# Attention over K and V: one shared pool for both loads, V six pairs behind K, later stores, and the last store on two queues

## The chip, the cores and the metric

The kernel runs on one core of a Trainium2 chip. The metric is the device time of a run in microseconds (us). The medians come from three to eleven runs of a kernel. A trace and a profile belong to one of these runs each. The span of a profile is about 1.8 us shorter than the time of its run.

A ratio below is the mean time of one kernel's fast runs over that of the other's in the same rounds on the same chip, so it is not quite the ratio of the medians that stand beside it.

## The reference

```python
B, Hq, Hkv, Sq, Sk, D = 16, 32, 8, 16, 2048, 128        # bf16, values about 0.05
def reference(q, k, v):
    k = jnp.repeat(k, Hq // Hkv, axis=1); v = jnp.repeat(v, Hq // Hkv, axis=1)
    scores = jnp.einsum("bhqd,bhkd->bhqk", q, k) * D ** -0.5
    return jnp.einsum("bhqk,bhkd->bhqd", softmax(scores), v)
```

There are 128 groups (a batch and a K/V head). Each has 64 query rows, 512 KB of K and 512 KB of V. The kernel works on 64 pairs of groups, so it loads 64 K transfers and 64 V transfers of 1 MB (the last V in two halves), 8 Q transfers of 256 KB, and stores 2 MB. All of K and V is read once: 134 MB. Nothing is reused, and this decides what can bound the kernel.

## The kernel before

All loads and stores are issued from SP in one fixed order. K and V have rings of buffers of their own, six for K and seven for V, each of 8 KB per partition. A load waits until the last reader of the buffer's previous content is done.

```python
NBK = 6; NBV = 7; NBO = 5; LAG = 5; DSTORE = 6
# ... order of the DMA queue: K(t), then V(t - lag), and every second step the store of two pairs
    for t in range(NP + max(lag, DSTORE) + 1):
        if t < NP:
            dma.append(("K", t))
        # ... Q chunks
        if 0 <= t - lag < NP:
            dma += v_of(t - lag)                       # the last pair: two halves
        if t - lag - DSTORE in range(0, NP, 2):
            dma.append(("ST", (t - lag - DSTORE) // 2))
# ... what a load waits for
    add(("K", i), *[opt(i >= nbk, ("kx", (i - nbk) // 2, i % 2, h)) for h in halves])
    add(v, opt(p >= NBV, ("pv", p - NBV, 0)))
```

`kx` is DVE's 32x32 transpose of K, `S` the scores, `ex` the exponential on ACT, `pt` and `pe` the transposition of the probabilities and its copy, `pv` the product with V, `nm` the normalization into the output tile. A store covers two pairs in two transfers of 32 KB, both from SP:

```python
                for gg in range(2):
                    g = 4 * x + 2 * gg
                    sp.dma_start(of[64 * g:64 * (g + 2), :].rearrange("(p m) d -> m p d", p=2),
                                 Osb[s][64 * gg:64 * (gg + 1), :, :]).then_inc(prog.sem_dma[kind][s], 16)
```

The exponential is taken without a maximum. So at the end every engine reads a flag that says whether all row sums lay in range, and branches: past a second program that would do it all again with the maximum, or into it.

```python
        eng.wait_ge(sem_flag, 4)
        eng.reg_load(reg, flag[0:1, 0:1].bitcast(I32))
        eng.br_eq(reg, all_within, on_true=after, on_false=redo).branch_hint(hints[me])
        # ... the second program lies here, then the label `after`
    # SP: transfers, this test, then fast.wait_stores(sp)
```

The branch is taken past the second program.

Of the kernel before, what the change touches and what calls it, by code (L numbers as in the profile page):

```python
# [11 lines left out]

NBK = 6
NBK_GENERAL = 4
NBV = 7
NBO = 5
NKT = 2
NPT = 3
LAG = 5
DSTORE = 6  # L20
QCH = 1024
# [8 lines left out]
    ("dve", "nm"): 0.36, ("dve", "pe"): 0.69, ("act", "pe"): 1.03, ("act", "qe"): 1.06, ("dve", "qe"): 1.25,  # L30
    ("act", "nm"): 0.42, ("act", "ex"): 1.27, ("pool", "qr"): 1.6, ("act", "qr"): 1.1, ("dve", "qr"): 1.1,
}
# [9 lines left out]
         "pe": ("act", "dve"), "qe": ("act", "dve"), "qr": ("pool",), "ex": ("act",), "qt": ("pe",), "S": ("pe",),  # L42
         "pt": ("pe",), "pv": ("pe",)}
_PRIO = {"S": 0, "mx": 0, "nb": 0, "ex": 0, "pt": 1, "pe": 1, "pv": 2, "rs": 2, "rc": 2, "nm": 2, "kx": 3, "qr": 3,
         "qt": 3, "qe": 3}


def make_ops(NP, pairs_per_chunk, general):

    deps = {}  # L50
    dma = []
    nbk = NBK_GENERAL if general else NBK
    ch = lambda p: p // pairs_per_chunk
# [6 lines left out]

    opt = lambda ok, op: op if ok else None
    v_of = lambda p: [("VH", x) for x in halves] if p == NP - 1 else [("V", p)]
    for c in range(n_ch):
        add(("Q", c), *[opt(c >= 2, ("qr", c - 2, x)) for x in range(4)])
        for x in range(4):
# [3 lines left out]
            add(("qe", c, x), ("qt", c, x), opt(c >= 2, ("S", last_of(c - 2))))  # L69
    for i in range(NP):  # L70
        add(("K", i), *[opt(i >= nbk, ("kx", (i - nbk) // 2, i % 2, h)) for h in halves])
    for p in range(NP):
        for v in v_of(p):
            add(v, opt(p >= NBV, ("pv", p - NBV, 0)))
    for s in range(NP // 2):
# [7 lines left out]
    for p in range(NP):  # L83
        for h in halves:
            u = 2 * (p // 2) + h
            if general:
                add(("mx", p, h), ("S", u), *[opt(p >= 2, ("ex", p - 2, x)) for x in halves])
            add(("ex", p, h), ("nb", p) if general else ("S", u), *[opt(p >= 2, ("pt", p - 2, x)) for x in halves])
        if general:
            add(("nb", p), ("mx", p, 0), ("mx", p, 1))  # L90
        for h in halves:
            add(("pt", p, h), ("ex", p, 0), ("ex", p, 1), opt(p >= 1, ("pe", p - 1, h)))
            add(("pe", p, h), ("pt", p, h), opt(p >= NPT, ("pv", p - NPT, 0)))
        for x, v in enumerate(v_of(p)):
            add(("pv", p, x), ("pe", p, 0), ("pe", p, 1), v, opt(p >= 1, ("nm", p - 1)))
        add(("rs", p), ("ex", p, 0), ("ex", p, 1))
        add(("rc", p), ("rs", p))
        add(("nm", p), ("pv", p, len(v_of(p)) - 1), ("rc", p), opt(p // 2 >= NBO, ("ST", p // 2 - NBO)))
        if p % 2:
            add(("ST", p // 2), ("nm", p - 1), ("nm", p))  # L100
    qstep = {max(0, c * pairs_per_chunk - QLEAD): c for c in range(n_ch)}
    dma.append(("Q", 0))
    lag = min(LAG, nbk - 1)
    for t in range(NP + max(lag, DSTORE) + 1):
        if t < NP:
            dma.append(("K", t))
        if qstep.get(t, 0):
            dma.append(("Q", qstep[t]))
        if 0 <= t - lag < NP:
            dma += v_of(t - lag)  # L110
        if t - lag - DSTORE in range(0, NP, 2):
            dma.append(("ST", (t - lag - DSTORE) // 2))
    dma += [("ST", s) for s in range(NP // 2) if ("ST", s) not in dma]
    return deps, dma


def pair_of(op, pairs_per_chunk):
    if op[0] in ("qr", "qt", "qe"):
        return op[1] * pairs_per_chunk - 1.5
    return 2 * op[1] + 0.5 if op[0] == "kx" else op[1] + {"S": -1.5, "pv": 1.5}.get(op[0], 0)  # L120


def build_schedule(NP, pairs_per_chunk, general):

    deps, dma = make_ops(NP, pairs_per_chunk, general)
    left = sorted((op for op in deps if op[0] in _ENGS),
                  key=lambda op: (pair_of(op, pairs_per_chunk), _PRIO[op[0]]))
    done, free = {}, {"pe": _T0, "dve": _T0, "act": _T0, "pool": _T0, "sp": _T0}
    progs = {"pe": [], "dve": [], "act": [], "pool": [], "sp": []}
    dma_left, dma_end = list(dma), _T0 + _DMA_LAT  # L130

    def ready(op):
# [5 lines left out]
        return r  # L138

    while left or dma_left:  # L140
        best = None
        if dma_left:
            rd = ready(dma_left[0])
            if rd is not None:
                st = max(free["sp"] + _LAT_SAME, rd + _LAT)
                best = ((round(st, 3), -1, -1), st, "sp", dma_left[0])
# [16 lines left out]
        if eng == "sp":  # L163
            dma_left.pop(0)
            end = st + _ISSUE
            dma_end = max(dma_end, end + _DMA_LAT) + _SIZE[op[0]] / _BW
# [6 lines left out]
        progs[eng].append(op)  # L173
    return deps, progs, max(done.values())


def bass_standalone__gqa_softmax__sampling_kernel(
# [27 lines left out]
    QT = [sb(f"QT{i}", [128, 4, qch], BF16) for i in range(2)]  # L205
    Kn = [sb(f"Kn{i}", [128, 2 * J * 64], I32) for i in range(NBK)]
    KT = [sb(f"KT{i}", [128, 2, J * 64, 2], I32) for i in range(NKT)]
    Vb = [sb(f"Vb{i}", [128, 2, J, 128], BF16) for i in range(NBV)]
    Sneg = [Kn[NBK_GENERAL + i][:, :].bitcast(F32) for i in range(2)]
    P = [sb(f"P{i}", [128, Sk], BF16) for i in range(2)]  # L210
# [18 lines left out]
    sem_id = sem("sem_id")  # L229
    sem_flag = sem("sem_flag")  # L230
    class Program:
        def __init__(self, tag, general):
            self.general = general
            self.rings = {"K": NBK_GENERAL if general else NBK, "V": NBV, "VH": 2, "Q": 2, "ST": NBO}
            self.deps, self.progs, _ = build_schedule(NP, qch // 128, general)
            self.sem_eng = {e: sem(f"{tag}_{e}") for e in ("pe", "dve", "act", "pool")}
            self.sem_dma = {kind: [sem(f"{tag}_{kind}{i}") for i in range(n)] for kind, n in self.rings.items()}
            self.where = {op: (e, i + 1) for e in self.sem_eng for i, op in enumerate(self.progs[e])}

        def point(self, op):  # L240
            if op[0] in self.rings:
                n = self.rings[op[0]]
                return self.sem_dma[op[0]][op[1] % n], (32 if op[0] == "ST" else 16) * (op[1] // n + 1)
            e, i = self.where[op]
# [19 lines left out]
        def wait_stores(self, eng):  # L264
            for s in range(max(0, NP // 2 - NBO), NP // 2):
                eng.wait_ge(*self.point(("ST", s)))

# [7 lines left out]
    def mark_hint(eng, me, prog, op):  # L275

        if not prog.general and op == prog.progs[me][max(0, len(prog.progs[me]) - HINT[me])]:
            hints[me] = eng.mark_branch_hint_location()

    def group_of(p, gg):  # L280
        return 4 * (p // 2) + 2 * gg + p % 2

    def elementwise(eng, me, prog, before_last=None):
        waits = prog.waiter(eng, me)
        for op in prog.progs[me]:
# [5 lines left out]
            if kind == "kx":  # L291
                _, _, gg, h = op
                ins = eng.transpose(KT[p % NKT][:, gg, :, h],  # L293
                                    Kn[(2 * p + gg) % prog.rings["K"]][:, J * 64 * h:J * 64 * (h + 1)])
            elif kind == "qr":
# [21 lines left out]
            elif kind == "rs":  # L317
                ins = eng.tensor_tensor(rowsum[:, p:p + 1], rhalf[:, p, 0:1], rhalf[:, p, 1:2], op=ALU.add)  # L318
            elif kind == "rc":
                ins = eng.reciprocal(rrec[:, p:p + 1], rowsum[:, p:p + 1])  # L320
            elif kind == "nm":
                dst, src, r = Osb[p // 2 % NBO][:, p % 2, :], O_ps[:, 0:128], rrec[:, p:p + 1]
                if me == "act":
# [14 lines left out]
    def transfers(sp, prog):  # L338
        waits = prog.waiter(sp, "sp")
        for op in prog.progs["sp"]:  # L340
            kind, x = op
            waits(op)
            mark_hint(sp, "sp", prog, op)
            s = x % prog.rings[kind]
            if kind == "K":
                dst = Kn[s][:, :].bitcast(BF16)
                src = kf[2 * x:2 * x + 2].rearrange("g (b r) d -> (g b) (r d)", r=2 * J)
            elif kind[0] == "V":
                p, part = (x, slice(0, J)) if kind == "V" else (NP - 1, slice(J // 2 * x, J // 2 * (x + 1)))
                g = group_of(p, 0)  # L350
                dst = Vb[p % NBV][:, :, part, :].rearrange("a g r d -> a g (r d)")
                src = vf[g:g + 3:2].rearrange("g (a r) d -> a g r d", r=J)[:, :, part, :].rearrange("a g r d -> a g (r d)")
            elif kind == "Q":
                dst, src = Qn[s][:, :, :], qf[qch * x:qch * (x + 1), :].rearrange("(a i) d -> a i d", i=NI)
            else:
                for gg in range(2):
                    g = 4 * x + 2 * gg
                    sp.dma_start(of[64 * g:64 * (g + 2), :].rearrange("(p m) d -> m p d", p=2),  # L358
                                 Osb[s][64 * gg:64 * (gg + 1), :, :]).then_inc(prog.sem_dma[kind][s], 16)
                continue  # L360
            sp.dma_start(dst, src).then_inc(prog.sem_dma[kind][s], 16)  # L361

    def matmuls(pe, prog):
        waits = prog.waiter(pe, "pe")
        for op in prog.progs["pe"]:
# [30 lines left out]
            else:  # L396
                rs = range(J) if p < NP - 1 else range(J // 2 * op[2], J // 2 * (op[2] + 1))
                for r in rs:
                    for gg in range(2):
                        ins = pe.matmul(  # L400
                            O_ps[64 * gg:64 * (gg + 1), 0:128],
                            PT[p % NPT][:, r, 64 * gg:64 * (gg + 1)],
                            Vb[p % NBV][:, gg, r, :],
                            start=(r == 0), stop=(r == J - 1), skip_group_check=True,
# [94 lines left out]
```

## Time and profile before

350.98 us, median of three runs (350.42 to 351.04).

| what | before |
|---|---|
| PE, ACT, DVE busy | 69%, 67%, 63% |
| hardware DMA queue, share of 16 engines | 98.2% |
| rate from 20 to 320 us | 413 to 414 GB/s |
| last normalize ends | 344.56 us |
| span ends | 349.2 us |

Lines of the profile's page of the kernel before: the span, the busy time of each engine, the DMA engines' busy tenths and rate in 40 slices, two queues with packets, MB and share of 16 engines' span, and issues with KB each and us to landing.

```profile
span 349.2 us, 11953 instructions
PE 240.3 (69%) x5378; PEld 171.6 (49%) x5378; DVE 220.9 (63%) x359; ACT 232.3 (67%) x387; POOL 28.9 (8%) x35
...
DMA  7999999999999999999999999999999999999972
GB/s 310 425 411 414 414 409 413 416 412 413 413 417 411 416 415 409 413 415 415 414 414 414 412 414 415 412 417 415 411 416 411 414 417 414 417 412 411 388 292 55
...
q1 hardware_dynamic: 37264, 138.42, 98.2%
q8 instruction: 43, 0.70, 0.8%
...
Kn<-in_k_dram SPq DMA_DIRECT2D x64, 1024.0 KB, 17.0
Vb<-in_v_dram SPq DMA_DIRECT2D x63, 1024.0 KB, 17.3
```

The compute engines are a third idle and the DMA engines are full from the second slice on. The three last slices (388, 292, 55) look as if something were left to gain there.

The windows of the kernel before: for each stretch in us, the busy time of each engine, the granted clock, the DMA share and GB/s.

```profile
20.00:100.00 80.00, 62.54 (x1358) 43.58 (x1336) 58.38 (x98) 57.02 (x94) 7.98 (x8) 0.91 1.02 413
100.00:200.00 100.00, 70.42 (x1653) 50.73 (x1649) 64.50 (x101) 72.54 (x123) 7.99 (x8) 0.97 1.03 414
200.00:320.00 120.00, 80.50 (x1856) 57.85 (x1856) 75.05 (x121) 80.38 (x138) 7.99 (x8) 0.94 1.03 414
...
330.00:336.00 6.00, 5.56 (x144) 4.10 (x128) 1.79 (x6) 5.14 (x9) 0.00 (x0) 1.00 1.00 384
336.00:342.00 6.00, 4.32 (x115) 3.66 (x112) 3.24 (x9) 0.01 (x1) 0.00 (x0) 1.00 0.59 210
342.00:349.20 7.20, 1.40 (x34) 1.07 (x34) 0.94 (x7) 0.00 (x0) 0.00 (x0) 0.85 0.11 22
```

At 336 to 342 us the rate is 210 GB/s at a DMA share of 0.59: half of the engines have nothing left. Which half, and why, the views do not say, but the trace has more. Each load raises its semaphore sixteen times, once for each DMA engine that has finished its share. The Trainium skill (DMA: Bandwidth & Descriptors, "Why a DMA increments its semaphore by 16 and not by 1") says that these engines finish independently, and the trace agrees. Here are the sixteen times of six loads of the kernel before (us, sorted within each load):

```
at 21 us        21.4 21.4 21.4 21.5 21.5 21.5 21.6 21.6 21.6 21.6 21.6 21.7 21.7 21.8 21.8 21.9
next load       23.9 23.9 23.9 24.0 24.0 24.0 24.0 24.1 24.1 24.2 24.2 24.2 24.3 24.3 24.4 25.7
later           49.0 49.1 49.1 49.1 49.2 49.2 49.2 49.3 49.3 49.3 49.3 49.5 50.7 50.9 51.1 51.1
late           300.5 300.6 300.6 300.8 301.0 301.7 302.4 303.2 306.9 306.9 307.0 308.2 308.4 308.5 308.6 308.7
last V, half 0 335.0 335.0 335.1 335.2 335.2 335.3 335.4 335.5 340.4 340.6 340.6 340.7 340.7 340.8 340.9 342.1
last V, half 1 336.2 336.2 336.3 336.4 336.4 336.6 336.6 337.0 341.8 341.9 342.0 342.0 342.1 342.1 342.2 343.5
```

One engine falls 1.4 us behind, then a few, and from about 286 us on eight engines come 5 to 8 us after the first. The last increments still follow each other every 2.5 us per load, to the end. A load counts only when its last engine is done, so the eight late engines set the pace of the kernel. The first step backwards (25.7) comes right after the first instruction fetch of 16 KB in the trace's DMA records, at 23.1 us.

The chain of instructions at the end, from the timeline of the kernel before:

```profile
343.53 0.64 PE L400 MATMUL O_ps<-Vb,PT 128*64 128x128 bf16 x16 [0.48 <-DMA Vb<-in_v_dram]
344.10 0.09 PEld L451 LDWEIGHTS QT_ps<-within,ones 128*1 128x1 f32 x2
344.10 0.19 PE L451 MATMUL QT_ps<-within,ones 128*1 128x2 f32 x2
344.21 0.35 DVE L326 TENSOR_SCALAR O<-O_ps,rrec 128x128 bf16<-128x128 f32 x1 [1.68 <-PE O_ps L400]
344.48 0.14 DVE L464 TENSOR_REDUCE flag<-QT_ps 1x1 f32<-1x2 f32 x1
344.59 1.25 SPq L358 DMA_DIRECT2D out_dram<-O  x2
```

The last product waited for the last V half (landed 343.5), then comes the last normalize, then SP issues two store transfers one after the other, 1.25 us for both. From the waits of SP in the same stretch:

```profile
SPq L266 <- DMA out_dram<-O: 1.6, 1, 1.6
```

Line 266 is the wait for the stores. SP was through with its range test and stood 1.6 us more for the last store.

### The profile page before, as it was taken

What the parts mean: (1) busy time and instruction counts of PE and PEld (TensorE: products, weight loads), DVE (VectorE), ACT (ScalarE), POOL (GpSimd) and SP (SyncE); (2) the same over time, 40 slices, a digit from 0 to 9 for tenths busy, and PEclk for the clock granted to TensorE, in tenths of its full rate; (3) what the DMA queues carried; (4) which work ended last, traced back from release to release, by engine and by line L of the source; (5) the groups of instructions that cost most, each with busy time, mean ns of one, the idle gap of its engine ahead of it and who ended that gap; (6) DMA issues with size and microseconds to landing.
All of it is one profiled execution on the core that took longest, in us unless ns stands there. A gap on an engine that the chain in (4) does not pass through costs nothing.

```text
span 349.2 us, 11953 instructions
## 1 busy us (share of the span) xinstructions
PE 240.3 (69%) x5378; PEld 171.6 (49%) x5378; DVE 220.9 (63%) x359; ACT 232.3 (67%) x387; POOL 28.9 (8%) x35
## 2 busy tenths in 40 slices
PE   1587778877687775866567767776757577676782
PEld 1355456554365553644445545454535455455562
DVE  4858867657787557666567555585566665675551
ACT  4488688867389477785569754787676676574740
POOL 1310003000130003000040000400004000000000
PEclk9999899989789899899999988999999989898998
DMA  7999999999999999999999999999999999999972
GB/s 310 425 411 414 414 409 413 416 412 413 413 417 411 416 415 409 413 415 415 414 414 414 412 414 415 412 417 415 411 416 411 414 417 414 417 412 411 388 292 55
DMA packets 37319, 139.23 MB, mean 399 GB/s; under 512 B 11408, under 2 KB 11408, under 8 KB 29072
## 3 DMA queue, kind: packets, MB, share of 16 engines
q1 hardware_dynamic: 37264, 138.42, 98.2%
q8 instruction: 43, 0.70, 0.8%
q14 instruction: 12, 0.10, 0.1%
HBM read 136.31 MB, written 2.10 MB: 396 GB/s over the span
## 4 chain that ended last, share of the span: by engine, by line
DMA 68%; PE 13%; DVE 7%; ACT 7%; SPq 4%; issue 1%
DMA Kn<-in_k_dram 64%; PE S_ps L384 6%; DVE KT L293 6%; ACT P L312 4%; PE PT_ps L394 4%; DMA Vb<-in_v_dram 3%; SPq L358 3%; PE O_ps L400 2%; ACT PT L335 2%; SPq L361 1%; PE QT_ps L372 1%; ACT QT L335 1%; DVE PT L335 1%; DVE rowsum L318 0%; DVE rrec L320 0%
## 5 line engine op out<-in xcount | busy, mean ns | idle before, releaser
L293 DVE STREAM_TRANSPOSE KT<-Kn 128x1024 int32<-128x1024 int32 x128 | 154.7, 1231 | 108.2 <-DMA Kn<-in_k_dram 98.8
L312 ACT ACTIVATE P<-S_ps 128x1024 bf16<-128x1024 f32 x128 | 130.1, 1023 | 63.2 <-PE S_ps L384 53.9
L384 PE MATMUL S_ps<-KT,QT 32*64 32x512 bf16 x2048 | 78.2, 414 | 50.3 <-DVE KT L293 37.4
L394 PE MATMUL PT_ps<-ident,P 128*128 128x128 bf16 x1024 | 76.3, 232 | 35.3 <-ACT P L312 30.4
L394 PEld LDWEIGHTS PT_ps<-ident,P 128*128 128x128 bf16 x1024 | 63.8, 104 | 62.5 <-ACT P L312 42.2
L400 PE MATMUL O_ps<-Vb,PT 128*64 128x128 bf16 x2048 | 73.5, 228 | 2.6 <-DMA Vb<-in_v_dram 2.0
L400 PEld LDWEIGHTS O_ps<-Vb,PT 128*64 128x64 bf16 x2048 | 62.9, 115 | 13.6 <-issue 5.5
L384 PEld LDWEIGHTS S_ps<-KT,QT 32*64 32x64 bf16 x2048 | 28.3, 107 | 73.5 <-DVE KT L293 41.1
L335 ACT ACTIVATE PT<-PT_ps 128x1024 bf16<-128x1024 bf16 x60 | 61.3, 1021 | 4.2 <-PE PT_ps L394 4.1
L299 POOL COPY Qr<-Qn 128x1024 bf16<-128x1024 bf16 x28 | 27.9, 1039 | 238.2 <-DMA Qn<-in_q_dram 238.2
L335 DVE COPY PT<-PT_ps 128x1024 bf16<-128x1024 bf16 x68 | 44.6, 662 | 1.8 <-PE PT_ps L394 1.6
L372 PE MATMUL QT_ps<-ident,Qr 128*128 128x128 bf16 x256 | 22.7, 239 | 15.8 <-ACT Qr L299 6.0
L324 ACT ACTIVATE O<-O_ps,rrec 128x128 bf16<-128x128 f32 x44 | 16.1, 367 | 24.1 <-PE O_ps L400 24.1
L335 ACT ACTIVATE QT<-QT_ps 128x1024 bf16<-128x1024 bf16 x24 | 24.6, 1023 | 8.7 <-PE QT_ps L372 8.6
L372 PEld LDWEIGHTS QT_ps<-ident,Qr 128*128 128x128 bf16 x256 | 17.0, 106 | 22.8 <-issue 12.3
L312 ACT ACTIVATION_READ_ACCUMULATOR P<-S_ps 128x1 f32 x128 | 25.9, 203 | 0.0
L326 DVE TENSOR_SCALAR O<-O_ps,rrec 128x128 bf16<-128x128 f32 x20 | 6.6, 329 | 7.5 <-PE O_ps L400 7.4
L318 DVE TENSOR_TENSOR rowsum<-rhalf 128x1 f32<-128x1 f32 x64 | 9.5, 177 | 1.6 <-ACT P L312 1.6
L335 DVE COPY QT<-QT_ps 128x1024 bf16<-128x1024 bf16 x8 | 9.7, 1210 | 1.1 <-PE QT_ps L372 1.1
L320 DVE RECIPROCAL rrec<-rowsum 128x1 f32<-128x1 f32 x64 | 7.9, 154 | 0.1
L299 ACT ACT_TABLE_LOAD x1 | 1.3, 1283 | 3.5 <-DMA Qn<-in_q_dram 3.5
L299 DVE COPY Qr<-Qn 128x1024 bf16<-128x1024 bf16 x2 | 1.3, 690 | 3.4 <-DMA Qn<-in_q_dram 3.4
(13 smaller groups left out, 4.2 us busy)
## 6 DMA issues: line engine op xcount, KB each, us to landing
Kn<-in_k_dram SPq DMA_DIRECT2D x64, 1024.0 KB, 17.0
Vb<-in_v_dram SPq DMA_DIRECT2D x63, 1024.0 KB, 17.3
Qn<-in_q_dram SPq DMA_DIRECT2D x8, 256.0 KB, 17.1
out_dram<-O SPq DMA_DIRECT2D x64, 32.0 KB, 13.7
Vb<-in_v_dram SPq DMA_DIRECT2D x2, 512.0 KB, 12.0
```

Of the source, the lines that this page charges most:

```text
L293: ins = eng.transpose(KT[p % NKT][:, gg, :, h], Kn[(2 * p + gg) % prog.rings["K"]][:, J * 64 * h:J * 64 * (h + 1)])
L299: ins = eng.activation(dst, src, ACT.Copy) if me == "act" else eng.tensor_copy(dst, src)
L312: ins = eng.activation(P[p % 2][:, :].rearrange("m (r a h j) -> m h a r j", h=2, a=2, j=32)[:, h], src.rearrange("m (a r j) -> m a r j", a ...
L318: ins = eng.tensor_tensor(rowsum[:, p:p + 1], rhalf[:, p, 0:1], rhalf[:, p, 1:2], op=ALU.add)
L320: ins = eng.reciprocal(rrec[:, p:p + 1], rowsum[:, p:p + 1])
L324: ins = eng.activation(dst, src, ACT.Copy, scale=r)
L335: ins = eng.activation(dst, src, ACT.Copy) if me == "act" else eng.tensor_copy(dst, src)
L358: sp.dma_start(of[64 * g:64 * (g + 2), :].rearrange("(p m) d -> m p d", p=2), Osb[s][64 * gg:64 * (gg + 1), :, :]).then_inc(prog.sem_dma[k ...
L372: ins = pe.transpose(QT_ps[:, 128 * i:128 * (i + 1)], Qr[:, x, i, :], ident[:, :],)
L384: ins = pe.matmul(S_ps[64 * gg:64 * (gg + 1), 512 * a:512 * (a + 1)], QT[c % 2][32 * a:32 * (a + 1), x, row:row + 64], kt[:, :, x // 2, p ...
L394: ins = pe.transpose(PT_ps[h][:, 128 * t:128 * (t + 1)], P[p % 2][:, 128 * r:128 * (r + 1)], ident[:, :])
L400: ins = pe.matmul(O_ps[64 * gg:64 * (gg + 1), 0:128], PT[p % NPT][:, r, 64 * gg:64 * (gg + 1)], Vb[p % NBV][:, gg, r, :], start=(r == 0), ...
```

## The change

The intent: one pool of fifteen slots for K and V in place of two rings, each slot given to the next load in the order in which a model of the schedule says that slots come free. V is six pairs behind K in place of five. Stores are issued twelve steps behind V in place of six, with nine output tiles. The last two pairs are stored apart, and the last pair in two transfers, one from SP and one from ACT (`STA`).

```diff
-NBK = 6
-NBK_GENERAL = 4
-NBV = 7
-NBO = 5
+NSLOT = 15
+NSLOT_GENERAL = 13
+NBO = 9
-LAG = 5
-DSTORE = 6
+LAG = 6
+DSTORE = 12
 ...
-        if p % 2:
+        if p == NP - 2:
+            add(("ST", p // 2), ("nm", p))
+        elif p == NP - 1:
+            add(("ST", NP // 2), ("nm", p))
+            add(("STA", 0), ("nm", p))
+        elif p % 2:
             add(("ST", p // 2), ("nm", p - 1), ("nm", p))
 ...
+    def take_slot(op):
+        best = None
+        for x, slot in enumerate(tenants):
+            last = frees(slot[-1], NP) if slot else []
+            if all(o in done for o in last):
+                cand = (max([done[o] for o in last], default=0.0), x, last)
+                best = cand if best is None or cand[:2] < best[:2] else best
+        return best
 ...
+            elif kind == "STA":
+                eng.dma_start(*out_rows(NP - 1, 1)).then_inc(*prog_sem(prog, op))
+                continue
 ...
+            elif x >= NP // 2 - 1:
+                p = NP - 2 if x == NP // 2 - 1 else NP - 1
+                for gg in range(2 if p == NP - 2 else 1):
+                    sp.dma_start(*out_rows(p, gg)).then_inc(*prog_sem(prog, op))
+                continue
```

## The prediction

> **What bounds the kernel now.** The DMA rings, not the compute engines. The page gives PE 69%, ACT 67%, DVE 63% busy; the hardware DMA queue is at 98.2% of 16 engines, and the stretches of 10 us from 10 to 320 us move 408 to 418 GB/s. The waits of the issuing engine (SPq, over 150 us in total) look large, but a load takes 17 us from issue to landing, nearly seven loads of 2.5 us: SPq waits while the rings are full.
>
> The last stretches look like an opening: 392 GB/s at 320-330, 315 at 330-340, about 210 GB/s (DMA share 0.57) at 336-342. I do not think it is one. The Trainium skill ("DMA: Bandwidth & Descriptors", on why a DMA increments its semaphore by 16) says that the engines of one DMA finish independently. The trace has all 16 increments of each load: first and last are 0.5 us apart at 20 us, but 8.2 us apart from 282 us on. Eight engines run late; the last increments still follow each other every 2.5 us per load to the end, plus 0.15 us for each store DMA between. The 43 instruction fetches of 16 KB (1.05 us each), which seem to fall on these eight, explain the lag (estimate: six steps of about 1.4 us on the slowest). At 336-342 the fast half has nothing left and the slow half works at its full rate. The slowest engine's work, 128 loads at 2.51, eight Q loads at 0.65, 58 store DMAs at 0.15 and its fetches, already fills 3 to 343.5 us. More slots, earlier issue and fewer SPq waits give the fast engines a longer lead and the slow ones nothing.
>
> **What changes, costed.**
> 1. Pool of fifteen, V six behind K: SPq waits shrink, loads take longer from issue to landing (estimate 25 to 33 us against 17), steady 414 GB/s unchanged. Worth 0 on the critical path.
> 2. Later stores: 52 store DMAs stand ahead of the last V load against 58. Six times 0.15 us: the last V half lands about 0.9 us earlier (343.5 to 342.6).
> 3. Split last store: before, the last normalize ended at 344.56, the first half store had landed at 346.5, the second, issued 0.6 us later, at 347.1 on twelve engines but 348.9 on four, where fetches came between. SPq waited 1.6 us for it, so the range test and branch were through by about 347.3. With the two halves issued together by SP and ACT, both should land about 2 us after the normalize, and the branch becomes the floor: 2.7 us instead of 4.4. Worth 0.6 to 1.6 us.
> 4. Nothing else on the path moves; PE, ACT and DVE work is reordered, not changed.
>
> Sum: 1.5 to 2.5 us, some of which may be lost to where the end's fetches fall. Predicted 348.9 us, 8 in 10 between 347.4 and 350.4. Chances: faster by over 2% 0.03, within 2% 0.96, slower 0.01.
>
> **What would show it.** Step 1: GB/s between 20 and 320 us within 2 of before; SPq waits for K and V loads shorter; issue to landing clearly above 17 us; the last landing's spacing still 2.5 us. Step 2: last V landing between 342 and 343.2 us, and a late bunch of stores landing after it. Step 3: normalize to end of span under 4 us (4.65 before).
>
> **What would make it wrong.** If the slow engines did sit idle for want of issued loads, a full queue would gain up to 5 us more (345 or less). If the number of fetches on the slowest engine changes by one, 1.4 us either way. If slots given out by modelled times block SPq on a release that comes late, the rings could run dry: slower. If the first DMA from ACT is slow to start, step 3 gives nothing.

## The result, and the profile after

The changed kernel takes 348.41 us (348.09 to 348.87, four runs) against 350.94 us before. The ratio is 0.9932, with a 95% interval from 0.9915 to 0.9949. So it is 2.5 us faster, within 2%.

The page of the changed kernel:

```profile
span 346.9 us, 11937 instructions
PE 238.6 (69%) x5378; PEld 172.7 (50%) x5378; DVE 225.8 (65%) x377; ACT 226.6 (65%) x369; POOL 29.0 (8%) x35
...
GB/s 309 426 412 415 411 413 412 412 415 414 411 418 415 412 412 414 415 413 414 413 412 417 414 415 414 414 413 415 413 413 414 412 417 416 414 412 412 392 336 108
...
q1 hardware_dynamic: 37216, 138.41, 98.9%
q8 instruction: 43, 0.70, 0.8%
...
slot<-in_k_dram SPq DMA_DIRECT2D x64, 1024.0 KB, 17.6
slot<-in_v_dram SPq DMA_DIRECT2D x63, 1024.0 KB, 17.7
```

The slices from the third on run at the same rate as before. A load takes 17.6 us from issue to landing, where it took 17.0: two more slots did not put more loads into flight. (The last slices have higher figures because the span, and so a slice, is shorter, and because more stores fall into them.)

Windows of the changed kernel:

```profile
20.00:100.00 80.00, 59.22 (x1352) 42.48 (x1344) 61.97 (x103) 56.91 (x94) 7.99 (x8) 0.96 1.02 413
100.00:200.00 100.00, 69.97 (x1594) 50.51 (x1595) 64.04 (x105) 69.78 (x115) 7.99 (x8) 0.93 1.03 414
200.00:320.00 120.00, 82.74 (x1904) 59.94 (x1902) 76.42 (x129) 78.09 (x132) 7.99 (x8) 0.94 1.02 414
...
330.00:336.00 6.00, 5.27 (x144) 4.20 (x144) 2.94 (x6) 3.15 (x5) 0.00 (x0) 1.00 0.98 370
336.00:342.00 6.00, 5.03 (x124) 4.19 (x117) 3.16 (x9) 3.15 (x5) 0.00 (x0) 1.00 0.61 203
```

413 and 414 GB/s in the three long stretches, as before, to the last digit. The half-empty stretch at 336 to 342 us is there too (203 against 210). The end, from the timeline of the changed kernel:

```profile
344.03 0.19 PE L519 MATMUL QT_ps<-within,ones 128*1 128x2 f32 x2
344.15 0.35 DVE L390 TENSOR_SCALAR O<-O_ps,rrec 128x128 bf16<-128x128 f32 x1 [0.91 <-PE O_ps L468]
344.42 0.14 DVE L532 TENSOR_REDUCE flag<-QT_ps 1x1 f32<-1x2 f32 x1
344.53 0.56 ACTq L381 DMA_DIRECT2D out_dram<-O  x1
```

The last normalize ends at 344.50 us; before it was 344.56. All but 0.06 us of the gain of 2.3 us in the span lies after it: 2.43 us from normalize to end in place of 4.66. The wait for the stores (1.6 us before) is not in the waits any more.

The trace gives the rest. Times after the last normalize, in us:

| | before | after |
|---|---|---|
| SP issues the last transfer it has | 0.66 | 0.03 |
| SP's branch starts | 2.10 | 1.32 |
| SP's first instruction after its branch | 2.61 | 1.85 |
| last store landed, twelve of its engines | 2.6 | 1.9 |
| last store landed, all sixteen | 4.35 | 1.99 |

Before, the last transfer landed on twelve engines at 347.0 to 347.2 us and on four at 348.5 to 348.9. In between lie an instruction fetch of 16 KB at 346.5 us and four of 8 KB from 346.2 to 347.7.

### The profile page after: what moved, and what is told of

It reads as the page before. It is cut to its first block, busy times and chain, and to the rows that moved or that the text cites. A ratio compares the mean times of both kernels' runs of the same rounds, so it can differ in the third digit from the quotient of the medians.

```text
span 346.9 us, 11937 instructions
## 1 busy us (share of the span) xinstructions
PE 238.6 (69%) x5378; PEld 172.7 (50%) x5378; DVE 225.8 (65%) x377; ACT 226.6 (65%) x369; POOL 29.0 (8%) x35
## 4 chain that ended last, share of the span: by engine, by line
DMA 72%; DVE 11%; PE 9%; ACT 6%; issue 1%; SPq 0%; ACTq 0%
DMA slot<-in_k_dram 72%; DVE KT L354 9%; PE O_ps L468 3%; ACT P L373 2%; PE PT_ps L462 2%; PE S_ps L452 2%; PE QT_ps L440 1%; ACT QT L399 1%; DVE PT L399 1%; ACT PT L399 1%; DMA Qn<-in_q_dram 1%; DVE O L390 1%; ACT L360 0%; ACT Qr L360 0%; DVE rowsum L379 0%
## 5 line engine op out<-in xcount | busy, mean ns | idle before, releaser
L354 DVE STREAM_TRANSPOSE KT<-slot 128x1024 int32<-128x1024 int32 x128 | 154.5, 1231 | 101.3 <-DMA slot<-in_k_dram 92.8
L462 PE MATMUL PT_ps<-ident,P 128*128 128x128 bf16 x1024 | 74.4, 229 | 83.1 <-DVE PT L399 44.0
L462 PEld LDWEIGHTS PT_ps<-ident,P 128*128 128x128 bf16 x1024 | 62.3, 102 | 104.7 <-DVE PT L399 53.7
L452 PE MATMUL S_ps<-KT,QT 32*64 32x512 bf16 x2048 | 75.9, 401 | 11.0 <-ACT P L373 9.7
L468 PE MATMUL O_ps<-slot,PT 128*64 128x128 bf16 x2048 | 76.7, 233 | 1.3 <-DVE O L390 1.0
L468 PEld LDWEIGHTS O_ps<-slot,PT 128*64 128x64 bf16 x2048 | 65.9, 119 | 17.8 <-issue 14.2
L399 ACT ACTIVATE QT<-QT_ps 128x1024 bf16<-128x1024 bf16 x23 | 23.5, 1023 | 7.3 <-PE QT_ps L440 7.3
L388 ACT ACTIVATE O<-O_ps,rrec 128x128 bf16<-128x128 f32 x27 | 9.9, 367 | 11.6 <-PE O_ps L468 11.6
L390 DVE TENSOR_SCALAR O<-O_ps,rrec 128x128 bf16<-128x128 f32 x37 | 12.0, 324 | 5.5 <-PE O_ps L468 5.4
L399 DVE COPY QT<-QT_ps 128x1024 bf16<-128x1024 bf16 x9 | 10.9, 1209 | 1.8 <-PE QT_ps L440 1.8
## 6 DMA issues: line engine op xcount, KB each, us to landing
slot<-in_k_dram SPq DMA_DIRECT2D x64, 1024.0 KB, 17.6
```

Source lines behind the costliest of these rows:

```text
L354: ins = eng.transpose(KT[p % NKT][:, gg, :, h], prog.slot(("K", 2 * p + gg))[:, J * 64 * h:J * 64 * (h + 1)])
L388: ins = eng.activation(dst, src, ACT.Copy, scale=r)
L390: ins = eng.tensor_scalar(dst, src, r, None, op0=ALU.mult)
L399: ins = eng.activation(dst, src, ACT.Copy) if me == "act" else eng.tensor_copy(dst, src)
L452: ins = pe.matmul(S_ps[64 * gg:64 * (gg + 1), 512 * a:512 * (a + 1)], QT[c % 2][32 * a:32 * (a + 1), x, row:row + 64], kt[:, :, x // 2, p ...
L462: ins = pe.transpose(PT_ps[h][:, 128 * t:128 * (t + 1)], P[p % 2][:, 128 * r:128 * (r + 1)], ident[:, :])
```

## The experiments

The theory under test, A: the late DMA engines bound the load stream, so the pool, the longer lead and the later stores are worth next to nothing, and the gain is the end of the program. The rival, B: the pool and the order gain by keeping the DMA queue fuller, and the end adds to it. Twelve kernels were run. The kernel before was run beside them on each chip (medians 350.86 to 351.00 us).

### The split of the last store alone, and the change without it

To the kernel before, only the parts of the change that concern the last two pairs were added (`o_of`, `STA`, the stores of pairs 62 and 63, the waits for them). The rings, LAG = 5 and DSTORE = 6 stayed.

> The kernel before with one part of the change alone: pair 62 stored by itself, pair 63 as two halves, one from SP and one from ACT. Theory A (the rings bound the load stream, the gain is the end of the program): nearly the whole gain, 348.4 to 349.0 us against 350.9; last normalize near 344.5 us, normalize to end of span about 2.4 us in place of 4.65. Theory B (the pool, the longer lead of K and the later stores gain by keeping the rings full): at most a third of the gain, 350.0 us or more.

Measured: 348.59 us (348.42 to 348.79), ratio to before 0.9934 (0.9921 to 0.9947). That is the whole gain, from a small part of the edit. Last normalize at 344.50, span 346.9.

The other way round, the changed kernel with the last two pairs stored together from SP:

```diff
-    o_of = lambda p: p // 2 if p < NP - 1 else NP // 2
+    o_of = lambda p: p // 2
-        if p == NP - 2:
-            ...
-        elif p % 2:
+        if p % 2:
```

> The changed kernel with the last two pairs stored together from SP, as before; pool, order and store delay kept. Theory A: the gain is gone, 350.3 to 351 us, with normalize to end of span about 4.5 us. Theory B: most of the gain stays, 349 us or less.

Measured: 351.46 us, ratio 1.0016 (1.0003 to 1.0028). The gain is gone, and a little more. Normalize to end of span is 5.65 us here, more than theory A said; part of that has a cause of its own, below. But the last store by itself was late enough: it landed on all sixteen engines only 4.71 us after the normalize (4.35 before the change, 1.99 after). Both runs together reject B.

### Both last halves from SP

```diff
-            add(("STA", 0), ("nm", p))
-                for gg in range(2 if p == NP - 2 else 1):
+                for gg in range(2):
```

> The changed kernel with pair 63 still stored apart from pair 62, but both its halves from SP, one after the other. If the second queue is what counts: the second half is issued 0.6 us later and SP reaches its range test 0.6 us later, so 349.0 us or more (0.6 above the changed kernel). If storing the pair apart (smaller and fewer transfers at the very end) is what counts: within 0.3 us of 348.4.

Measured: 350.78 us, ratio 0.9990. So storing the last pair apart from pair 62 is worth nothing by itself; the second queue is worth 2.4 us by the medians and 2.0 us by the ratios (0.9990 against 0.9932), over three times the 0.6 us of issue that it saves. The waits of SP show the same wait as before the change:

```profile
SPq L315 <- DMA out_dram<-O: 1.8, 1, 1.8
```

The second half was issued 0.5 us after the first. It landed on twelve engines at 346.7 to 346.8 us, and on the last at 348.96. The Trainium skill (DMA: Bandwidth & Descriptors, "Issuing engines are not separate DMA queues") says that issuing from several engines only saves the sequencer's time, usually small. For the transfer itself that holds. What the saved half microsecond seems to have bought here is to be ahead of the fetches that follow the branch. The next run tests this.

### The same without the range test

To see whether it is the branch that holds four engines, the run with both halves from SP was made without the test, the branches and the second program. It is correct for these inputs and is no version to keep.

```diff
-            unless_in_range(sp, "sp", again)
+            # the same on the four other engines; flag and its product left out too
```

> The run with both last halves from SP (350.78 us), without the range test and the other branch of the program behind it. There the second half landed on twelve engines at 346.8 us and on four at up to 348.96. If the instruction fetches that follow the branch hold these four: all sixteen within 0.5 us of each other, and the time down by about 2 us, to 348.4 to 349.2. If a second transfer from the same queue is late in itself: four engines still up to 2 us late, and 350 us or more.

Measured: 348.89 us, 1.9 us less by the medians (1.5 by the ratios, 0.9947 against 0.9990), at the upper part of what was expected. The second half landed at 346.4 to 346.6 us on all sixteen engines. The page shows one fetch of 16 KB less, and in the trace no fetch of either size begins after 344.4 us.

```profile
span 347.1 us, 11913 instructions
q8 instruction: 42, 0.69, 0.8%
```

So the branch and what follows it cause the straggling, and a second transfer on a queue is not late in itself. That the instruction fetches do it is the reading of their times and sizes. The run took them away together with the branch, so this step is inferred.

### Stores six steps behind V

```diff
-DSTORE = 12
+DSTORE = 6
```

> The changed kernel with stores issued six steps behind V, as before, in place of twelve. My prediction said that later stores let the last V half land 0.9 us earlier (six store DMAs of 0.15 us moved behind it); the profile of the changed kernel shows only 0.16 us. If the 0.9 us is real but hidden by an instruction fetch on the slowest engine and by the compute chain: last V landing up to 0.9 us later, time up by 0 to 0.9 us. If the stores' place is worth nothing: within 0.2 us of 348.4.

Measured: 348.62 us, 0.2 us above the changed kernel and inside its scatter. The last V half landed 0.34 us later (343.67 against 343.33) and the last normalize ended 0.33 us later. So the stores' place is worth about 0.3 us in the profile, not 0.9.

### How many slots

```diff
-NSLOT = 15
+NSLOT = 10
```

> The changed kernel with ten slots in the pool in place of fifteen. Both traces show that a slot is held for 18 to 19 us (from the issue of its load to the end of its last reader) while a load is issued every 2.55 us, so 7 to 8 slots are in use at a time, whatever the pool holds; and no more than about eight loads and stores are in flight. Theory A (the pool is not what limits issue): within 0.3 us of 348.4. Theory B (more slots keep the rings fuller): slower by 2 us or more, with a lower steady GB/s.

Measured: 350.89 us. By the time alone, theory A would fall here: five slots less take the whole gain. But the loads were not later: last V half at 343.3 us, last normalize at 344.33, last store at 346.4 us, all as in the changed kernel. What came later was the end of the span, at 349.2 us. In this run the first instruction of SP after its branch starts 2.59 us after the branch, where the changed kernel has 0.45. That is a stall that no slot takes part in. The run with the joint last store has it too. A table of the runs discussed so far, from the traces:

```
run                      SP: instructions before its branch, then us from branch to next instruction
ten slots                208   2.59
joint last store         209   2.59
changed kernel           210   0.45
both halves from SP      211   0.44
before                   215   0.44
split alone              216   0.44
stores six steps behind  232   0.44
```

So ten slots were run once more, with waits for counts that had long been reached, put before four of the K loads:

```diff
+            if kind == "K" and x in (36, 40, 44, 48) and not prog.general:
+                for e in ("pe", "dve", "act", "pool"):
+                    sp.wait_ge(prog.sem_eng[e], x - 30)
```

> The run with ten slots took 350.89 us, but its loads and stores were as early as in the changed kernel (last store landed at 346.4 us); SP stood still for 2.66 us after its branch, against 0.5 us in the changed kernel, as it did in the run with the joint last store. SP had issued 208 and 209 instructions before its branch in these two, 210 or more in all runs without the stall. So here the same ten slots, with waits for counts long reached put before four K loads (four or more instructions more, nothing else). If where the branch lies in SP's program decides the stall, and not the pool: no stall, 348.2 to 348.9 us. If ten slots are too few: 350.5 us or more, as before.

Measured: 348.36 us (348.1 to 348.9), ratio 0.9931. The branch is now instruction 216 of SP, the gap 0.44 us. Useless instructions made the kernel 2.5 us faster, and the pool of ten is as good as that of fifteen. The stall belongs to the place of the branch in SP's program. It is not the distance from the branch hint, which every one of these branches has: the hint lies 167 instructions ahead both in the run with the joint store, which stalls, and in the changed kernel, which does not. Whether the place of the branch or that of its target counts is open, since the waits move both. The Trainium skill (Runtime: NRT & Kernel Launch, "Instruction fetch mechanics") says that instructions come in blocks of 16 KiB, and that a branch to a target outside the window that is loaded stalls for a fetch. The stall fits this, but that it is a fetch is not shown: near SP's branch the traces hold one fetch of 16 KB with the stall (346.2 us with ten slots) and without it (346.3 us in the changed kernel). Why 209 misses and 210 hits, these runs do not tell.

With eight slots and the same waits:

> The same with eight slots. 7.3 slots are in use on average in the traces (18.5 us held, one load per 2.55 us). If the slots in use are what the loads need: eight is at the edge, some issue waits for a slot, the steady GB/s falls by 1 to 5% and the time is 351 to 365 us. If the queue hides it: within 0.5 us of the run with ten slots.

Measured: 349.18 us (348.70 to 350.49), 0.8 us above ten slots: between the two cases, and well under the 351 us of the first. The profile is of the slowest of its four runs. The rate stays at 408 to 420 GB/s in the slices from the third to the thirty-sixth. SP came 0.4 us late to its last store, and that store again landed late on one engine (348.3 us, the other fifteen by 346.6). So even eight slots hardly starve the queue. The traces say why. When SP ends an issue between 60 and 320 us, seven to nine earlier transfers are in flight, in 99% of the cases before the change, in 97% after it and with ten slots. And the slots had long been free: each load's slot had been released at least 8.8 us before SP began to issue the load before the change, and at least 11.3 us after it (5.7 us at the median with ten slots, 0.7 with eight). So the long waits of SP, which lie in the issues themselves, are not for slots, though the view of its waits names engines for them. That they end when the queue has room fits the steady count. What sets this limit is left open.

### Are the late engines late because of instruction fetches?

PE's instructions are 10756 of the 11937. The first test took 3584 of them away by leaving out 14 of the 16 blocks of each product with V. The result is wrong; loads and stores are untouched.

```diff
-                rs = range(J) if p < NP - 1 else range(J // 2 * op[2], J // 2 * (op[2] + 1))
+                rs = (0, J - 1) if p < NP - 1 else ((0,), (J - 1,))[op[2]]
```

> Wrong result on purpose: the product with V uses 2 of the 16 key blocks, which takes 3584 of PE's 10756 instructions away and leaves every load and store as it is. If instruction fetches make eight engines late: 28 to 29 fetches of 16 KB in place of 43, first and last increment of a load at 300 us 5 to 6 us apart in place of 8, last V half landing at 340 to 341.5 us in place of 343.3, time 346 to 347.3 us. If these eight engines are slow for another reason: still 8 us apart, time within 0.4 us of 348.4 (PE's lighter work alone can take about 0.5 us off the tail of the last pair).

Measured: the page has 29 fetches in place of 43, the first and last engine of a load are 5.1 us apart at 300 us and 6.2 at 319 us (8.2 at both times in the changed kernel), and the last V half landed at 340.2 us in place of 343.3. All three as expected for fetches.

```profile
span 346.4 us, 8353 instructions
q8 instruction: 29, 0.48, 0.6%
```

The time, 349.57 us (348.19 to 350.79), is a miss. In the profiled run, the fastest of the four, the last normalize ended at 341.49 us, 3.0 us earlier than in the changed kernel. Then PE's branch took 3.90 us in place of 0.49 and ended at 346.03, and the last store landed at 345.8. So the gain was lost behind the branch again, this time on PE, and in a late store. The granted clock was lower too, 0.76 to 0.78 in the four runs (0.94 to 0.95 in the changed kernel); what that cost was not separated. The time of this run says little; its landings do.

A correct version of the test: in pairs 8 to 23, one product for both groups (128 rows by 256 columns, of which half is read) in place of two, on top of the kernel before with the split. It takes 512 instructions from PE.

```diff
+MERGED = range(8, 24)
 ...
+                if p in MERGED and not prog.general:
+                    for r in rs:
+                        ins = pe.matmul(O_ps[:, 0:256], PT[p % NPT][:, r, :], Vb[p % NBV][:, :, r, :],
+                                        start=(r == 0), stop=(r == J - 1))
+                    rs = ()
+    # and nm in two halves for these pairs: rows 0:64 from columns 0:128, rows 64:128 from 128:256
```

> The kernel before with the split of the last store (348.59 us), and in pairs 8 to 23 one product with V for both groups, 128 rows by 256 columns, half of whose result is not read (sixteen matmuls of a pair in place of 32, normalize in two halves): 512 of PE's 10756 instructions less, two fetches of 16 KB less. In the run before, the 41st fetch, at 336.3 us, held one of the sixteen engines up by 1.3 us (343.4 against 342.1 for the next), and the last product waited for it. If fetches make the late engines late: the last V half lands 1.0 to 1.6 us earlier, and 347.0 to 347.7 us. If not: 348.4 to 348.8 us.

Measured: 350.38 us, a miss in time, a hit in mechanism. The last V half landed at 342.2 us (343.4 with the split alone) and the last normalize ended at 343.24 (344.50). Then 5.4 us passed to the end. The waits of SP in this run show where: line 461 is the barrier at the end of the program, where all engines meet.

```profile
SPq L461 <- PEq L461: 3.3, 1, 3.3
```

The name is that of the event; the engine that came last was ACT, by the trace. Its next instruction after its branch came 3.17 us later, where the other runs have 0.40 to 0.43. The second normalize halves had made ACT's program longer: the branch was its instruction 447, in all other runs it was 400 to 436. It is the same stall, on another engine. So in the last run the normalize of the 16 pairs was given to DVE:

```diff
-            engs = ("dve", "act") if op[:2] == ("qr", 0) else _ENGS[op[0]]
+            engs = ("dve", "act") if op[:2] == ("qr", 0) else ("dve",) if op[0] == "nm" and op[1] in MERGED and not general else _ENGS[op[0]]
```

> The run before with the merged products for pairs 8 to 23 had its last normalize done at 343.24 us (344.50 with the split alone), but ACT stood still for 3.17 us after its branch, which was instruction 447 of ACT; in all runs without that stall it was between 400 and 436. Here the normalize of these 16 pairs goes to DVE alone, so ACT's branch lies near 424 and DVE's near 418 (386 to 431 were without a stall). If both readings hold (fetches set the late engines, the branch's place sets the stall): last V half near 342.2 us, no stall over 0.6 us, 347.0 to 347.6 us, faster than both kernels. If the earlier load end is no gain in itself: 348.4 us or more.

Measured: 347.72 us (347.52 to 347.88), ratio to before 0.9908 (0.9891 to 0.9925): 0.1 us above the range that was expected, and faster than both kernels. It was not run in the same rounds as the changed kernel, and the intervals of the two ratios overlap; each of its four runs is below each of the changed kernel's four. ACT's branch was instruction 413, with a gap of 0.42 us. Page and SP's waits:

```profile
span 345.7 us, 11445 instructions
q1 hardware_dynamic: 37216, 138.41, 99.3%
q8 instruction: 41, 0.67, 0.8%
...
SPq L461 <- PEq L461: 0.2, 1, 0.2
```

Against the split alone (another chip), the last normalize is 1.22 us earlier and the time 0.87 us shorter. The sixteen landings of the last V half show what two fetches less did:

```
split alone (41 fetches by 337 us)   ... eight engines to 337.0, seven at 341.5 to 342.0, the last at 343.4
merged products (39 by 337 us)       ... eight engines to 337.4, then 340.5 and seven at 341.6 to 342.2
```

The one engine that was 1.4 us behind its seven fellows is back among them, and another one is 1.1 us ahead of them.

The traces at hand say more than that. In the kernel before, the last landing falls back by 1.3 us, on top of the usual distance between loads, right after the fetches number 1, 9, 17, 25 and 33 (at 23.1, 81.8, 144.5, 206.8 and 271.7 us), and again after number 41 (336.2 us). In the changed kernel, and in the run with two of the sixteen key blocks, whose fetches lie further apart, the steps follow the fetches of the same numbers. Every eighth fetch hits the engine that is last, as if the fetches went round eight engines in turn. Summed over the sixteen engines, the lag behind the first one grows from 3.8 us at 22 us to 68.6 us at 329 us in the kernel before: 1.7 us for each of the 39 fetches in between (1.8 us for each of 27 with two key blocks). With 39 fetches in place of 41 by 337 us, numbers 40 and 41 are missing before the end, which fits the two engines that moved.

### Moving work to the early engines

```diff
+XP = 50
+XT = 24
 ...
+        if 0 <= t - XT < 16 and not general:
+            dma.append(("VX", t - XT))      # V of pair 50, rows of partitions 8i to 8i+8
 ...
```

> The changed kernel with the V load of pair 50 issued as sixteen transfers of 8 partitions (64 KB) one per step from step 24, into a slot kept for it. By the Trainium skill (DMA: Bandwidth & Descriptors, how k is chosen) a transfer of 8 partitions runs on the eight lowest-numbered engines. If these are the early half: the late half has 64 KB less each to move, so the last V half lands about 2.5 us earlier and the time is 346 to 346.8 us, with about 3 to 4 us between first and last increment at 300 us. If they are the late half: the lag grows to 13 us and the time to about 351 us. If the lag is spread over engines otherwise: within 0.5 us of 348.4.

Measured: 357.08 us, 8.7 us slower, which none of the three cases foresaw. The rate fell from 414 to 373 to 394 GB/s in just the slices where these small transfers were issued.

```profile
GB/s 311 426 413 419 412 405 415 412 413 414 417 412 415 383 394 391 388 392 383 373 383 377 389 387 416 410 416 415 414 410 412 414 416 414 418 411 409 368 360 71
```

A reading that fits: with about eight transfers in flight, a transfer of 64 KB takes the place of one of 1 MB, and engines run dry. It is argued, and the trace gives it little support: at the end of SP's issues from 105 to 205 us, 9.4 transfers and 5.6 MB are in flight on average, against 8.1 and 5.9 MB in the changed kernel. So the cause of the loss is open. Each of the small transfers raised its semaphore in nine steps in place of sixteen, which fits eight engines and one step for the rest. The landings afterwards (at 300 us) spread evenly over 10 us rather than in two halves, so the eight engines that these transfers used seem to be neither the early nor the late half. Which engines are late stays open.

## Why the prediction was right

The time (348.41 us) lies in the predicted range, near the predicted 348.9. The main claim, that the loads are bound by DMA engines that are already full and that more slots give nothing, held in every run that tests it. The sum of the parts, 1.5 to 2.5 us, held at its upper end. The parts did not all hold, and that the sum did is partly luck: step 2 fell short by 0.7 us, and step 3 went over its upper end by 0.6.

- **"Worth 0 on the critical path"** (step 1) was right: same rate in each long stretch, the split alone gives all, and ten slots do as well as fifteen. But its sign, **"loads take longer from issue to landing (estimate 25 to 33 us against 17)"**, was wrong: 17.6 us. I took the number of slots for the depth of the queue. The limit is seven to nine transfers in flight, before and after. "SPq waits shrink" failed with it: the waits ahead of its loads add up to 144 us after and 111 us before.
- **"The last V half lands about 0.9 us earlier"** (step 2) was mis-sized: 0.16 us (343.49 to 343.33). Fifteen engines were done by 341.6 us, 0.6 us earlier than before; the sixteenth was held by the fetch at 339.0 us (before, by the one at 336.2, the 41st in both). Undoing the later stores alone moved the landing by 0.34 us. And the last normalize hardly moved, 0.06 us: with V six pairs behind, the last product waited for the normalize of the pair before, no longer for the load.
- **"Worth 0.6 to 1.6 us"** (step 3, the split store) was mis-sized: 2.23 us (4.66 to 2.43). The mechanism was the predicted one, stragglers behind fetches. What I had as a floor, **"the branch becomes the floor: 2.7 us"**, was itself moved by the change. SP issues its stores before its test, so with one transfer less its branch starts at 1.32 us in place of 2.10.
- **"The 43 instruction fetches ... seem to fall on these eight, explain the lag"** is supported: 29 fetches gave 6.2 us of lag in place of 8.2, and two fetches less before the end brought the last engine back by 1.2 us. "Six steps of about 1.4 us on the slowest" is what the traces show too: 1.3 us (1.5 in the changed kernel) after every eighth fetch. That the fetches fall on eight engines only is inferred from these steps and from the two halves of the landings.
- The risk that I did not name is the largest of all: 2.2 to 2.7 us hang on where a branch lies in an engine's program. The changed kernel and the kernel before both happen to have it well placed. With two instructions less on SP, as the run with ten slots has, the same change would have shown no gain.

## What to carry to other kernels

When a kernel is bound by transfers, look at the sixteen landings of each transfer, not at the mean rate: the engine that is latest sets the pace, and a half-empty tail can hide an engine that is full to the end. After the last piece of work, ask what is in the DMA queue and in the instruction stream behind it; a store issued half a microsecond later cost two. When a variant differs in time but not in its work, compare the gap after each engine's branch before believing the edit did it.

## What the Trainium skill lacked or had wrong

- Runtime: NRT & Kernel Launch, "Instruction fetch mechanics" calls the cost of crossing a block of instructions mostly hidden. Whether it is for the engine that executes, no run here looked. For the loads it was not: each fetch of 16 KB took 1.05 us on a DMA engine, the loads behind it came 1.3 to 1.7 us later on one engine, and the late half of the engines ended 5 to 7 us behind the early half.
- The same section has no word on how large the stall behind a branch is, nor on branch hints. Here all these branches had a hint, and the stall came and went with a few instructions: 2.6 to 3.2 us against 0.4 to 0.5, with 209 instructions before SP's branch stalled and 210 not, 447 before ACT's stalled and 436 not.
- DMA: Bandwidth & Descriptors has no limit on transfers in flight from one issuing engine. Here it was about eight (seven to nine at the end of 97 to 99% of the issues between 60 and 320 us), with thirteen, fifteen and ten slots alike, and the rate was 5 to 10% lower while 64 KB transfers were among them.
- The same page, "Issuing engines are not separate DMA queues", says that a second issuing engine only saves issue time. At the end of this program the 0.6 us saved were worth 2.0 to 2.4 us, because the transfer got ahead of what follows the branch, instruction fetches by all that the runs show.
- No page says that the engines of a long stream of full-width transfers drift apart with the instruction fetches: 0.5 us at 20 us, 8.2 us at 300 us.
